# Local-and-global attention and a gated feed-forward on one core: key tiles of 120 + 8, stationary V, half-batches and hand-ordered streams in place of key blocks of 128, whole batches and the tool's order

## Chip, cores and metric

One core of one Trainium2 chip. The metric is the device time in microseconds of one execution, as the median of several; each comparison runs the two kernels in turn on the same chip. A profile is one execution with the hardware profiler; its span is some 1.7 us shorter than that execution's time.

## The reference

```python
# q, k, v: [4 batches, 8 heads, 768 tokens, 64]; n_global = 8, n_local = 96
scores = q @ k.T / 8
keep   = (key < 8) | (0 <= query - key < 96)
bias   = -slope[h] * (96 if global and not local else |query - key|)
a      = softmax(where(keep, scores + bias, -1e9))
x      = (a @ v), as [3072 tokens, 512]
out    = (relu(x @ w_gate) * (x @ w_val)) @ w_out     # 512 -> 1536 -> 512
```

Inputs and output are float32; both kernels compute in bfloat16 with float32 sums. The bias enters as a product with a table of exponentials after the exponential of the score, and the row sum comes from ones beside V, in the same matmuls as the values.

## The kernel before

Attention runs by batch and head pair. Scores of a 128-key block against the 256 queries that can see it go into one PSUM bank with a second block; the values come from `es` as the stationary operand and V (with a column of ones) as the moving one, so x has tokens on partitions and is transposed back. The feed-forward runs in chunks of 512 tokens, each as soon as its batches are done.

```python
f1g_psum = tile_pool(name="f1g", bufs=1, space=PSUM)      # one bank each
f1v_psum = tile_pool(name="f1v", bufs=1, space=PSUM)
f2_psum  = tile_pool(name="f2ps", bufs=1, space=PSUM)
# ... cut
for hp in range(H // 2):
    attention_pair(b, hp, x_sb, qkts[hp], vss[hp])
    # ... loads cut
    if hp < len(ffn_chunks):
        ffn_chunk(ffn_chunks[hp])                          # a whole chunk after one pair
bridge_batch(b, x_sb)                                      # transposes x
# ... cut; in ffn_chunk:
for fc in range(12):
    psg = f1g_psum.tile(...); psv = f1v_psum.tile(...)
    # 4 matmuls of 512 columns into psg, 4 into psv
    nc.scalar.activation(grelu, psg, Relu)
    nc.vector.tensor_tensor(ht[:, fc, :], psv, grelu, op=mult)
for tt in range(4):
    ps2 = f2_psum.tile(...)                                # 12 matmuls of 512 columns
    nc.scalar.copy(osb, ps2)
```

The chunks that become ready number 1, 2, 1 and 2 after batches 0 to 3, so batch 1 and batch 3 have one chunk beside their attention, and the last two chunks run alone.

The softmax here doesn't subtract the row's maximum and nothing guards it: scores larger than these inputs give would overflow.

## Time and profile before

| | before |
|---|---|
| time, median of 4 | 338.35 us |
| span of the profiled run | 339.5 us |
| busy: TensorE, VectorE, ScalarE, GpSimd | 298.9, 159.2, 127.2, 75.3 us |
| mean granted clock | 0.95 |
| DMA packets, bytes | 81,159, 20.77 MB |

Read it so: TensorE is the engine that the others serve, but its busy time is the sum of overlapping and modelled matmul durations, so 88% busy does not say that 12% is all there is to gain. The prediction below therefore builds a floor from the distances between the starts of matmuls, and shows the lines. The profiled execution is not one of the four timed: with a span of 339.5 us it took some 341, so it was about 1% slower than the median.

### The profile page before, as it was taken

The numbers are of one execution on the slowest core, as the hardware profiler recorded it, in microseconds if no ns is written. First come the engines' busy times: TensorE is split into PE (matmuls) and PEld (weight loads), VectorE is DVE, ScalarE is ACT, GpSimd is POOL, SyncE is SP. The second block draws the span as 40 slices with busy tenths as digits, with TensorE's granted clock in tenths as the row PEclk, the third lists the DMA queues.
The fourth block names the chain that finished last, engine by engine and source line by source line (L and its number), as shares of the span: only waits on it lengthen the run. The fifth ranks groups of instructions, "written<-read, shape, count | busy, mean of one in ns | idle before, by whom it ended". The sixth has DMA issues, their size and how long they took to land.

```text
span 339.5 us, 4809 instructions
## 1 busy us (share of the span) xinstructions
PE 298.9 (88%) x1858; PEld 145.1 (43%) x1888; DVE 159.2 (47%) x405; ACT 127.2 (37%) x233; POOL 75.3 (22%) x93
## 2 busy tenths in 40 slices
PE   0499878899997698999899997999998799999984
PEld 0254454544444354444444454544444343444431
DVE  8977676444258555422533266833366233113300
ACT  3356605232366242234332562432565133223311
POOL 9993192998011611000100000000000000000000
PEclk9999999599999959999999999999995599999999
DMA  6999999999317973001400110000210000020011
GB/s 41 118 136 200 195 163 181 150 140 132 78 62 48 71 47 23 0 33 62 56 0 2 64 61 2 0 2 0 75 50 0 2 0 1 32 93 1 0 57 69
DMA packets 81159, 20.77 MB, mean 61 GB/s; under 512 B 75504, under 2 KB 77040, under 8 KB 81136
## 3 DMA queue, kind: packets, MB, share of 16 engines
q0 software_dynamic: 77680, 14.16, 51.6%
q1 hardware_dynamic: 3456, 6.29, 5.0%
q8 instruction: 15, 0.25, 0.3%
q14 instruction: 8, 0.07, 0.1%
HBM read 28.31 MB, written 6.29 MB: 102 GB/s over the span
## 4 chain that ended last, share of the span: by engine, by line
PE 69%; DMA 10%; POOL 8%; DVE 5%; issue 4%; ACT 2%; DVEq 0%; POOLq 0%; ACTq 0%
PE f1v_ps L305 20%; PE f_ps L316 18%; PE f1g_ps L299 16%; DMA wv_sb<-in_moe_w_val_dram 6%; PE qk_ps L190 4%; DMA qs<-in_q_dram 4%; POOL qs L79 3%; POOL ks L80 3%; PE qk_ps L195 3%; PE tp L100 2%; PE av_ps L222 2%; DVE ht L312 2%; ACT es L201 2%; POOL vs L82 2%; PE tp L256 1%
## 5 line engine op out<-in xcount | busy, mean ns | idle before, releaser
L312 DVE TENSOR_TENSOR ht<-f1v_ps,grelu 128x512 bf16<-128x512 f32 x72 | 49.7, 691 | 81.5 <-PE f1v_ps L305 77.1
L311 ACT ACTIVATE grelu<-f1g_ps 128x512 bf16<-128x512 f32 x72 | 43.0, 598 | 113.5 <-PE f1g_ps L299 102.7
L305 PE MATMUL f1v_ps<-xt_all,wv_sb 128*128 128x512 bf16 x276 | 77.9, 390 | 4.5 <-DVE ht L312 3.8
L299 PE MATMUL f1g_ps<-xt_all,wg_sb 128*128 128x512 bf16 x276 | 78.0, 392 | 3.2 <-DVE xt_all L261 1.9
L201 ACT ACTIVATE es<-qk_ps 128x512 bf16<-128x512 f32 (+1 forms) x128 | 67.7, 571 | 29.3 <-PE qk_ps L195 26.3
L316 PE MATMUL f_ps<-wo_sb,ht 128*128 128x512 bf16 x282 | 65.2, 379 | 2.3 <-ACT osb L321 2.1
L305 PEld LDWEIGHTS <-wv_sb 128*128 128x128 bf16 x288 | 28.2, 99 | 45.3 <-issue 22.6
L190 PE MATMUL qk_ps<-dst 64*128 64x256 bf16 x128 | 38.7, 317 | 5.0 <-ACT es L201 3.2
L316 PEld LDWEIGHTS <-ht 128*128 128x128 bf16 x288 | 27.9, 98 | 34.0 <-issue 2.9
L299 PEld LDWEIGHTS <-wg_sb 128*128 128x128 bf16 x288 | 28.4, 101 | 31.6 <-issue 4.3
L195 PE MATMUL qk_ps<-dst 64*128 64x256 bf16 (+1 forms) x128 | 37.1, 305 | 0.0
L321 ACT COPY osb<-f_ps 128x512 f32<-128x512 f32 x24 | 14.1, 586 | 56.6 <-PE f_ps L316 36.0
L79 POOL DMA_DIRECT2D qs<-in_q_dram x34 | 30.3, 891 | 15.5 <-DMA wo_sb<-in_moe_w_out_dram 6.8
L82 POOL DMA_DIRECT2D vs<-in_v_dram x16 | 17.3, 1080 | 65.8 <-PE av_ps L235 36.3
L80 POOL DMA_DIRECT2D ks<-in_k_dram x34 | 30.1, 888 | 6.8 <-DMA wg_sb<-in_moe_w_gate_dram 6.6
L222 PE MATMUL av_ps<-vs,es 128*128 128x65 bf16 x192 | 23.9, 215 | 2.3 <-DVE x_sb L246 2.0
L204 DVE TENSOR_TENSOR es<-es,m_gg 128x512 bf16<-128x512 bf16 x64 | 22.8, 382 | 5.4 <-ACT es L201 5.1
L204 DVE TENSOR_TENSOR es<-es,m_kg 128x512 bf16<-128x512 bf16 x32 | 13.4, 418 | 25.4 <-ACT es L201 24.9
L104 DVE COPY dst<-tp 128x768 bf16<-128x768 bf16 x32 | 17.7, 552 | 12.8 <-PE tp L100 12.8
L222 PEld LDWEIGHTS <-es 128*128 128x128 bf16 x192 | 15.8, 109 | 17.7 <-issue 6.6
L228 PE MATMUL av_ps<-vs,es 128*128 128x65 bf16 x160 | 21.3, 214 | 0.0
L100 PE MATMUL tp<-ident,qs 128*128 128x128 bf16 x96 | 10.4, 257 | 12.4 <-DMA qs<-in_q_dram 10.8
(40 smaller groups left out, 180.0 us busy)
## 6 DMA issues: line engine op xcount, KB each, us to landing
out_dram<-osb SPq DMA_DIRECT2D x24, 256.0 KB, 2.0
vs<-in_v_dram POOLq DMA_DIRECT2D x16, 192.0 KB, 4.8
qs<-in_q_dram POOLq DMA_DIRECT2D x30, 96.0 KB, 4.3
ks<-in_k_dram POOLq DMA_DIRECT2D x30, 96.0 KB, 4.2
wg_sb<-in_moe_w_gate_dram POOLq DMA_DIRECT2D x1, 1536.0 KB, 12.7
wv_sb<-in_moe_w_val_dram POOLq DMA_DIRECT2D x1, 1536.0 KB, 19.3
wo_sb<-in_moe_w_out_dram POOLq DMA_DIRECT2D x1, 1536.0 KB, 13.5
qs<-in_q_dram POOLq DMA_DIRECT2D x4, 48.0 KB, 2.6
```

Source lines behind the costliest of these rows:

```text
L79: nc.gpsimd.dma_start(out=qs[:, sl, e, :], in_=src_q[:, sl])
L80: nc.gpsimd.dma_start(out=ks[:, sl, e, :], in_=src_k[:, sl])
L190: nc.tensor.matmul(ps[:, 0:colsA], lhsT=kT[:, blkA[0] * 128 : blkA[0] * 128 + 128], rhs=qT[:, blkA[1] : blkA[2]], start=True, stop=False)
L195: nc.tensor.matmul(ps[:, colsA : colsA + colsB], lhsT=kT[:, blkB[0] * 128 : blkB[0] * 128 + 128], rhs=qT[:, blkB[1] : blkB[2]], start=Fals ...
L201: nc.scalar.activation(es[:, 0:cols], ps[:, 0:cols], AF.Exp, bias=0.0, scale=scale)
L204: nc.vector.tensor_mul(es[:, 0:cols].rearrange("p (a c) -> p a c", a=2), es[:, 0:cols].rearrange("p (a c) -> p a c", a=2), m2[:, h, 0:cols ...
L222: nc.tensor.matmul(dst(qt), lhsT=lhs, rhs=vsl[:, qt, :], start=(cnt[bank] == 0), stop=False)
L299: nc.tensor.matmul(psg, lhsT=wg_sb[:, dc, fc * 128 : (fc + 1) * 128], rhs=xt_all[:, dc, t0 : t0 + TCH], start=(dc == 0), stop=(dc == N_DC ...
L305: nc.tensor.matmul(psv, lhsT=wv_sb[:, dc, fc * 128 : (fc + 1) * 128], rhs=xt_all[:, dc, t0 : t0 + TCH], start=(dc == 0), stop=(dc == N_DC ...
L311: nc.scalar.activation(grelu, psg, AF.Relu, bias=0.0, scale=1.0)
L312: nc.vector.tensor_tensor(ht[:, fc, :], psv, grelu, op=ALU.mult)
L316: nc.tensor.matmul(ps2, lhsT=ht[:, fc, tt * 128 : (tt + 1) * 128], rhs=wo_sb[:, fc, :], start=(fc == 0), stop=(fc == N_FC - 1))
```

## The change

Intent, part by part:

- **Key tiles.** A tile holds 8 global and 120 local keys, so one score matmul per tile and head pair covers both kinds; q is laid out with the other head's half zero, so one matmul serves two heads.
- **V and ones stationary.** `es` streams past V; x comes out with features on partitions, as the feed-forward wants it. The transposes of x go. The row sum arrives on 64 partitions, and its reciprocal is made on ScalarE as exp(-log(sum)).
- **Half-batches of 384 tokens.** Attention of half c+1 is cut into pieces and spread between the feed-forward pieces of half c.
- **Rotating banks.** Gate, value and output groups share three banks in turn.
- **Hand-ordered streams.** `manual_schedule()`: each engine executes in the order in which the program names its instructions; before, the tool's scheduler chose.
- **Wide rows.** q and k come in as float32 in runs of 768 bytes (three tokens), through the SP queue, and are cast on GpSimd (q of half 0 on VectorE); before, GpSimd's queue cast while it moved runs of 64 elements.

```diff
+    QH = S // 2; NN = 3; KT = 128 - NG; NHALF = 2 * B
-    f1g_psum ... bufs=1;  f1v_psum ... bufs=1;  f2_psum ... bufs=1
+    ff_psum = tile_pool(name="ffps", bufs=3, space=PSUM)
+    ctx.enter_context(tc.manual_schedule())
...  (loads)
-                nc.gpsimd.dma_start(out=qs[:, sl, e, :], in_=src_q[:, sl])
+            nc.sync.dma_start(out=dst[:, h0:h1, :],
+                in_=src[b, h0:h1, half*QH:(half+1)*QH, :].rearrange("h (p n) d -> p h (n d)", n=NN))
...  (values: es stationary, V moving -> V stationary, es moving)
-                nc.tensor.matmul(dst(qt), lhsT=es[...], rhs=vsl[:, qt, :], ...)
+            nc.tensor.matmul(av3[:, :, a : a + w], lhsT=vb[:, j, z0 : z0 + 128], rhs=es[...], ...)
+        nc.scalar.activation(ln[o0:o0+64], av[d0:d0+64, 0:QH], AF.Ln)
+        if e == 1:
+            nc.scalar.activation(rc, ln, AF.Exp, scale=-1.0)
+            for e_ in range(2):
+                nc.vector.tensor_tensor(xT_of[s][r, p, :], av_of[s, p, e_][r, 0:QH], rc[r], op=mult)
...  (order of the attention pieces of one half)
+        return (C(0) + C(1) + T(0) + C(2) + T(1) + C(3) + QK(0) + T(2) + QK(1) + AV(0) + T(3) + QK(2) + AV(1)
+                + QK(3) + AV(2) + AV(3))
...  (after the attention of half 0)
+    nc.vector.memset(vbuf[1]..., 0x3F803F80)               # ones of the second V buffer
+    # zero columns of the key tiles: 12 small memsets
+    for c in range(NHALF):
+        if c + 2 < NHALF:
+            load_half(c + 2)
+        a_items, f_items = attention_pieces(c + 1), ffn_pieces(c)
+        # after each feed-forward piece, as many attention pieces as are due
```

C is a cast, T the transposes of one head pair, QK a bank of scores, AV one head's values. Cuts are marked by "...".

Words used below. A PSUM bank is a piece of the memory in which TensorE leaves its sums. A *half* is one half-batch; there are eight, numbered from 0. A *group* is the set of matmuls that fill one bank once. The *product* is VectorE's multiplication of a value group with the relu of its gate group; it empties the value bank. The *normalisation* is VectorE's multiplication of a head pair's values with the reciprocal of their row sums. A *fill* is a memset that writes constant ones or zeros into a buffer.

## The prediction

> **What bounds the kernel now.** I read the page's slices first, then the chain, the windows on either side of the first feed-forward matmul, the groups, and last the timelines of two stages.
>
> ```profile
> PE   0499878899997698999899997999998799999984
> PEclk9999999599999959999999999999995599999999
> DMA  6999999999317973001400110000210000020011
> ...
> PE 69%; DMA 10%; POOL 8%; DVE 5%; issue 4%; ACT 2%; DVEq 0%; POOLq 0%; ACTq 0%
> ```
>
> TensorE is busy nearly everywhere and makes up 69% of the chain; the other engines do not bound. But the first quarter is DMA-busy, and the granted clock falls to half in slices near 60, 120 and 255 us. The same split, cut where the first gate matmul begins (48.7 us):
>
> ```profile
> 0.00:48.00 48.00, 31.62 (x244) 18.41 (x246) 37.74 (x138) 21.38 (x41) 34.53 (x46) 1.00 1.51 140
> 48.00:339.50 291.50, 267.32 (x1619) 126.71 (x1645) 121.50 (x267) 105.84 (x192) 40.81 (x48) 0.94 0.42 48
> ```
>
> PE busy is not PE at its peak, so I made a floor from start-to-start times at full clock: 12 output matmuls of 512 columns take 2.59 us (0.2158 each), two neighbouring score matmuls of 256 columns start 0.11 us apart, value matmuls of 65 columns 0.030, and 128-column transposes I take as 0.056 (estimate, from the column rate). Floor before: feed-forward 864 x 0.2158 = 186.4; scores 61,440 columns 26.2; values 480 x 0.030 = 14.5; 288 transposes (q, k, and x back) 16.1; together 243. The span is 339.5, so 96 us is lost: about 34 before 48.7 us, 58 after, 3.6 of tail. How the middle loses it, in the last chunk, which runs alone:
>
> ```profile
> 320.95 1.03 PE L299 MATMUL f1g_ps<-xt_all,wg_sb 128*128 128x512 bf16 x4
> 321.22 0.69 DVE L312 TENSOR_TENSOR ht<-f1v_ps,grelu 128x512 bf16<-128x512 f32 x1 [1.18 <-PE f1v_ps L305]
> ...
> 325.62 0.59 ACT L321 COPY osb<-f_ps 128x512 f32<-128x512 f32 x1 [3.00 <-PE f_ps L316]
> ...
> 326.25 2.75 PE L316 MATMUL f_ps<-wo_sb,ht 128*128 128x512 bf16 x11 [0.68 <-ACT osb L321]
> ```
>
> One value bank: the value group may begin only after the product has emptied it. The pair repeats every 1.87 us against 8 x 0.2158 = 1.73, so 72 x 0.15 = 10 us. One output bank: after every 12 matmuls TensorE waits 0.68 us for the copy, up to 24 x 0.7 = 16 us where no attention fills it. The rest is attention of whole batches with only one chunk beside it (98 to 127 us, 198 to 219, 248 to 268), data waits near 60 and 120 us, and the half clock these bring.
>
> The start:
>
> ```profile
> DMA packets 81159, 20.77 MB, mean 61 GB/s; under 512 B 75504, under 2 KB 77040, under 8 KB 81136
> ...
> 27.64 0.95 POOL L79 DMA_DIRECT2D qs<-in_q_dram  x1
> 35.24 0.82 POOL L80 DMA_DIRECT2D ks<-in_k_dram  x1 [6.64 <-DMA wg_sb<-in_moe_w_gate_dram]
> ```
>
> Nearly all packets are small. And GpSimd's issue at 35.24 waits for the transfer issued eight issues earlier; so do those at 42.23 and 58.61. I read eight as the number it may have open.
>
> **What the Trainium skill says.** "TensorE: Matmul & The Clock Gate", "Back-to-back issue gap": N/2.4 + 2.5 ns per matmul; the trace's 0.2158 at N=512 agrees, so I use it for 384 columns (0.1625). The same page, "Part 1: The HAM clock gate": a TensorE idle for a window drops to half clock; the 5s in the clock row stand where TensorE has gaps, so this agrees. "DMA: Bandwidth & Descriptors", "Specifications": transfers want 512 bytes for full rate; here 118 GB/s in the slice of 128-byte q, k, v packets against 209 in that of weights, which agrees. "GPSIMD Engine Reference", "4.1 Engine selection": one-input work there is roughly at line rate; no run here shows it, and I need it for the casts.
>
> **The change, part by part.**
> *TensorE work.* Feed-forward: 8 halves x 96 matmuls x 0.1625 = 124.8, plus 288 output matmuls 62.2: unchanged. Scores: the tile overlaps give 200 + 232 token columns in units of three, for two heads 1,200 columns in a first half and 1,392 in a second; 41,472 in all, 17.3 us + 144 x 2.5 ns = 17.6 (8.6 less). Values: V is stationary, so the moving side is es, again 41,472 columns: 17.3 + 288 x 2.5 ns + the shortest at a floor = 18.4, that is 4 *more* than before. Transposes: x leaves attention already transposed, 192 remain, 10.7 (5.4 less). Floor after 234: only 10 us less. **The gain must come from the 96 us of loss.**
>
> *Steady state.* One half is 29.2 us of TensorE: feed-forward 23.4 (24 x 0.65 + 6 x 1.3), attention of the next half 5.9. Three rotating banks remove the two waits above: a group takes 0.65 us, and its bank returns after about 0.2 + 0.56, within two groups.
> Is another engine slower? From durations here (ACT 167 ns + 0.84 per element; DVE from PSUM f32 551 ns at 384, bf16 masks 352 ns at 384):
> ACT per half: 12 relu 5.9, 3 output copies 1.8, 12 exponentials 6.4, 8 logarithms 3.9, 4 reciprocals as exponentials 2.1, 4 k copies 1.7: 21.8.
> DVE: 12 products 6.7, 18 mask products 5.4, 8 q copies 2.8, small k copies 1.5, 8 normalisations 4.4: 20.8.
> Both below 29.2. But the 12 products lie in the first two thirds of a half: DVE there is 17.2 of 19.7 us, tight. One wait I can point to: the last two head pairs' value pieces stand one output piece (1.3 us) apart, with two banks; logarithm 0.49, exponential 0.52, two products 1.1 plus hand-overs need about 2.2: 0.9 us lost per half. With 0.7 for jitter: 30.8 per half. Seven halves: 215.6.
>
> *Start.* q and k now come through SP in 768-byte runs; the first two loads should land within 4 us. But order is kept: GpSimd issues 13 transfers (about 1 us each, as now) after VectorE has filled the V buffer (3,808 words; memsets of 64 and 128 words took 112 and 165 ns, so 3.2 us, done at about 4.3), and only then casts k. First cast at about 17 us, first transpose at 18. VectorE's fills, mask arithmetic (14 operations near 0.3) and q cast end near 12, so they hide. Then half 0 runs with nothing beside it, in ScalarE order: 12 exponentials 6.4, logarithms and reciprocals 6.0, k copies 1.7, 12 late mask exponentials of 216 elements at about 0.38 (4.6), waits between: some 23 us, to 41. Second-buffer fills on VectorE (about 4.5 us) then delay the first product; three banks cover 1.9: feed-forward starts in effect at 43.7. So **the start hardly shrinks** (48.7 before), although only half a batch is waited for.
>
> *End.* The last half alone, 23.6, then copy and store 3.6, as now.
>
> Sum: 43.7 + 215.6 + 23.6 + 3.6 = **286 us**.
>
> **Rivals.**
> (a) VectorE or ScalarE becomes the bound. For: 87% of the first two thirds; strict program order makes one late item stall both; casts on GpSimd may slow VectorE. Against: averages of 71 to 75%, and the present timeline shows back-to-back ScalarE operations at no extra cost. At 34 us per half: 309.
> (b) The start is longer: casts on GpSimd behind a stalled issue. For: the eight-open rule; the weight transfers took 12 to 19 us to land. Against: the 13th issue waits for a V load, not for weights. If it waited for weights, 10 us more: 296.
> (c) The hand order works almost perfectly: 29.5 per half, and half 0 overlaps better, start 36: 270.
> (d) Nothing gained: the present loss is hidden structure that returns as waits. I see no wait large enough; 50 us would have to come back.
>
> **Range and chances.** (a) and (b) pull up, (c) down; half (a) and half (b) give about 302. I choose 286, range 270 to 305. Being within 2% needs (a) and (b) both in full and more: faster 0.96, same 0.03, slower 0.01.
>
> **What will show it.** In the changed profile: gate and value groups 0.65 us apart, with no wait of TensorE on the product; 512-column output groups with no 0.68 wait; seven repeats of 30 to 32 us; clock row at 9 from the first feed-forward on; first transpose near 18 us behind GpSimd's k cast; first gate matmul near 41. Wrong if: TensorE idles behind VectorE or ScalarE for over 3 us in a half, the value matmuls start much further apart than columns/2.4, or ScalarE shows table loads beyond the first.

## The result

| | before | after |
|---|---|---|
| time, median of 4 | 338.35 us | 304.6 us |
| span of the profiled run | 339.5 us | 302.9 us |
| busy: TensorE, VectorE, ScalarE, GpSimd | 298.9, 159.2, 127.2, 75.3 us | 247.9, 169.1, 168.3, 60.9 us |
| DMA packets, bytes | 81,159, 20.77 MB | 51,208, 27.50 MB |

The ratio of fast runs is 0.899 (95% interval 0.896 to 0.903). A ratio here is the mean time of one kernel's fast runs over that of the other's in the same rounds, so it is not quite the ratio of the medians quoted. The time lies inside the range (270 to 305), at its upper edge, 18.6 us above the predicted 286; 1.7 of that is only that the prediction added up a span. So the mechanism held and two terms of the sum were too small; a second chip gave the changed kernel 307.8. Bytes are counted as written, so q and k, which now arrive as float32, count double; both kernels read 28.3 to 28.4 MB.

Slices, and the first line of the chain, of the kernel after:

```profile
PE   0025351998899889989898989988998899899995
PEclk9999999999999999999999999999999999999999
DMA  3999999905192614432760518001700110001002
...
PE 69%; DVE 12%; ACT 10%; POOL 3%; DMA 3%; issue 3%; ACTq 0%; POOLq 0%
```

From the ninth slice on the TensorE row has no lump and the clock row no 5. The first eight slices are worse than before. In the chain GpSimd and DMA have given place to VectorE and ScalarE. The same cut in time as the prediction's, for the kernel after (columns: stretch, its length, busy time of TensorE, weight loads, VectorE, ScalarE, GpSimd, clock, DMA, GB/s):

```profile
0.00:48.00 48.00, 16.03 (x84) 9.48 (x84) 27.33 (x76) 19.72 (x47) 14.67 (x25) 1.00 1.12 200
48.00:302.90 254.90, 231.84 (x1581) 138.51 (x1596) 141.80 (x402) 148.57 (x314) 46.27 (x80) 1.00 0.35 70
```

TensorE did half as much in the first 48 us as before, and 254.9 us remain instead of 291.5. The last half, which runs alone, from TensorE's timeline of the kernel after:

```profile
289.50 0.81 PE L363 MATMUL ff_ps<-xT,wvB 128*128 128x384 bf16 x4
290.15 0.81 PE L353 MATMUL ff_ps<-xT,wgB 128*128 128x384 bf16 x4
290.81 0.81 PE L363 MATMUL ff_ps<-xT,wvB 128*128 128x384 bf16 x4
291.45 7.93 PE L372 MATMUL ff_ps<-wo_sb,ht 128*128 128x512 bf16 x35
```

Groups of four start 0.65 us apart, four times the 0.1625 that the prediction took, and all output matmuls follow in one run of 7.9 us without the 0.68 us wait. TensorE stands at its floor here.

**The books.** First gate matmuls of halves 1, 2 and later start at 84.64, 116.35, 148.39, ... 275.86 us: a mean period of 31.87 us. One period before 84.64 is 52.8, the start of half 0's feed-forward "in effect": when it would have begun had half 0 run at that period. With the prediction's floors:

| loss against TensorE's floor, us | before | after |
|---|---|---|
| start (to 48.7 / 52.8, less the attention's floor of 14.2 / 5.4) | 34.5 | 47.4 |
| middle | 58 | 18 |
| tail | 3.6 | 3.7 |
| floor itself | 243 | 234 |

So the 36.6 us of span come from the middle (-40) and the floor (some -9), and the start gives 13 back. The medians differ by 33.75 only; the other 3 us lie in the slow profile of the kernel before.

### The profile page after: what moved, and what is told of

Read it like the earlier page. It is cut to its first block, busy times and chain, and to the rows that moved or that the text cites. A ratio compares the mean times of both kernels' runs of the same rounds, so it can differ in the third digit from the quotient of the medians.

```text
span 302.9 us, 4741 instructions
## 1 busy us (share of the span) xinstructions
PE 247.9 (82%) x1665; PEld 148.0 (49%) x1680; DVE 169.1 (56%) x477; ACT 168.3 (56%) x361; POOL 60.9 (20%) x105
## 2 busy tenths in 40 slices
DMA packets 51208, 27.50 MB, mean 91 GB/s; under 512 B 27952, under 2 KB 46896, under 8 KB 51184
## 4 chain that ended last, share of the span: by engine, by line
PE 69%; DVE 12%; ACT 10%; POOL 3%; DMA 3%; issue 3%; ACTq 0%; POOLq 0%
PE ff_ps L372 20%; PE ff_ps L363 18%; PE ff_ps L353 17%; DVE xT L331 6%; PE av_ps L314 5%; PE qk_ps L286 5%; PE tp L245 3%; DMA vbuf<-in_v_dram 3%; ACT lnd L323 2%; ACT grelu L356 2%; ACT rcp L328 2%; POOL vbuf L135 2%; DVE ht L365 1%; DVE qp L251 1%; DVE vbuf L399 1%
## 5 line engine op out<-in xcount | busy, mean ns | idle before, releaser
L372 PE MATMUL ff_ps<-wo_sb,ht 128*128 128x512 bf16 x273 | 67.2, 379 | 0.8
L365 DVE TENSOR_TENSOR ht<-ff_ps,grelu 128x384 bf16<-128x384 f32 x96 | 53.1, 554 | 24.3 <-PE ff_ps L363 21.6
L331 DVE TENSOR_TENSOR xT<-av_ps,rcp 64x384 bf16<-64x384 f32 x64 | 35.5, 555 | 46.2 <-ACT rcp L328 33.5
L356 ACT ACTIVATE grelu<-ff_ps 128x384 bf16<-128x384 f32 x96 | 47.3, 493 | 24.3 <-DVE ht L365 13.8
L353 PE MATMUL ff_ps<-xT,wgB 128*128 128x384 bf16 x256 | 52.0, 325 | 4.8 <-DVE ht L365 4.8
L363 PE MATMUL ff_ps<-xT,wvB 128*128 128x384 bf16 x256 | 52.0, 325 | 3.5 <-ACT grelu L356 3.5
L289 ACT ACTIVATE es<-qk_ps 128x432 bf16<-128x432 f32 (+2 forms) x96 | 49.1, 538 | 4.0 <-PE qk_ps L286 3.2
L298 DVE TENSOR_TENSOR es<-es,m_all 128x432 bf16<-128x432 bf16 (+6 forms) x144 | 40.6, 314 | 18.1 <-ACT es L289 17.0
L286 PE MATMUL qk_ps<-qp,kT 128*128 128x432 bf16 (+6 forms) x144 | 33.6, 303 | 7.9 <-ACT es L289 7.9
L323 ACT ACTIVATE lnd<-av_ps 64x384 f32<-64x384 f32 x64 | 31.0, 485 | 12.8 <-PE av_ps L314 11.1
L234 POOL CAST qk<-qs 128x384 bf16<-128x384 f32 x28 | 14.3, 510 | 101.0 <-DMA qs<-in_q_dram 35.0
## 6 DMA issues: line engine op xcount, KB each, us to landing
wvB<-in_moe_w_val_dram POOLq DMA_DIRECT2D x1, 1024.0 KB, 29.5
```

Source lines behind the costliest of these rows:

```text
L286: nc.tensor.matmul(ps[:, c : c + n_], lhsT=kt[:, j, :], rhs=qd[:, :, :, a : a + w], start=True, stop=True)
L289: nc.scalar.activation(es[:, 0:cols], ps[:, 0:cols], AF.Exp, bias=0.0, scale=scale)
L298: nc.vector.tensor_mul(e4, e4, mk)
L323: nc.scalar.activation(ln[o0 : o0 + 64], av[d0 : d0 + 64, 0:QH], AF.Ln, bias=0.0, scale=1.0)
L331: nc.vector.tensor_tensor(xT_of[s][r, p, :], av_of[s, p, e_][r, 0:QH], rc[r], op=ALU.mult)
L353: nc.tensor.matmul(psg[:, 0:QH], lhsT=wg_of(dc, fc), rhs=xT[:, dc, :], start=(dc == 0), stop=(dc == N_DC - 1))
```

## Experiments

Each was run with a profile and three rounds against the kernel before on the same chip. The chips differ by a per cent. Kernels e1 to e4 share one chip, c0 to e7 another, e8 to e11 a third. All gave correct results. In c0 to e7 only two of the seven executions of the kernel before were fast, so ratios rest on two. The program that judges the runs calls the change and e8 to e11 faster, and c0 and e1 to e7 unclear; of all the intervals only that of e4 holds 1.

### What held the start

GpSimd's timeline of the kernel after:

```profile
17.21 1.02 POOL L152 DMA_DIRECT2D wo_sb<-in_moe_w_out_dram  x1 [0.85 <-DMA vbuf<-in_v_dram]
18.23 0.96 POOL L234 CAST qk<-ks 128x384 bf16<-128x384 f32 x2
20.08 0.96 POOL L234 CAST qk<-ks 128x384 bf16<-128x384 f32 x2 [0.90 <-DMA ks<-in_k_dram]
48.20 0.62 POOL L124 DMA_DIRECT2D vbuf<-in_v_dram  x1 [27.15 <-DVE vbuf L399]
48.81 3.61 POOL L135 DMA_DIRECT2D vbuf<-in_v_dram  x4
52.42 0.52 POOL L234 CAST qk<-qs 128x384 bf16<-128x384 f32 x1
```

and TensorE's, of the same kernel:

```profile
45.41 1.49 PE L353 MATMUL ff_ps<-xT,wgA 128*128 128x384 bf16 x4
52.99 0.94 PE L245 MATMUL tp<-ident,qk 128*128 128x128 bf16 x6 [6.09 <-POOL qk L234]
```

The first k cast came at 18.2 us, behind all 13 transfers, as foreseen. But then GpSimd stood for 27 us: its next instruction loads V of batch 1, and that waits for VectorE to fill the second V buffer, which the program names after the whole attention of half 0. The casts of half 1 stand behind that load, and TensorE idles 6.1 us for them.

**e1_early_fill.** The fills moved ahead of the first head pair:

```diff
     for h in range(2): build_masks(h)
+    nc.vector.memset(vbuf[1]..., 0x3F803F80); 12 small memsets
     pieces = attention_pieces(0)
     ...
-    nc.vector.memset(vbuf[1]..., 0x3F803F80); 12 small memsets
```

> The changed kernel with the second V buffer and the zero columns of the key tiles filled ahead of the first head pair instead of after the last one, in the stretch from 13 to 19 us where VectorE stands idle. Theory (the 8 us that the start lost against the prediction come from GpSimd's stream: the casts of half 1 stand behind a V load that waits for this fill, so TensorE idles 6.1 us at 47 us and the first product is late by some 3): 304.6 falls by 8 to 9, to about 296. Rival 1 (the start is bound by transfers; the slices are DMA-busy until 55 us): another wait takes its place, on q, k or weights, and it falls by under 3. Rival 2 (the fill itself on VectorE is the cost): falls by 3 to 4 only.

Measured 299.07 us, ratio 0.887 (0.879 to 0.895) against 0.899; span 297.0 against 302.9. That is 4 us by the ratios and 6 by the spans, less than the 8 to 9 expected. The idle is gone: the half-1 transposes start at 48.32 with no wait. But in this run the first k cast came at 19.94, not 18.23, since GpSimd's last two weight transfers waited 3.7 us for V loads to land instead of 1.6. With that 1.7 us the sum is 7.6. GpSimd's timeline of this run also shows what else can stand there:

```profile
26.88 0.93 POOL L135 DMA_DIRECT2D vbuf<-in_v_dram  x1 [3.03 <-DMA wvA<-in_moe_w_val_dram]
46.56 0.92 POOL L135 DMA_DIRECT2D vbuf<-in_v_dram  x1 [4.90 <-DMA wvB<-in_moe_w_val_dram]
53.88 0.64 POOL L135 DMA_DIRECT2D vbuf<-in_v_dram  x1 [6.39 <-DMA wo_sb<-in_moe_w_out_dram]
```

Each waits for the transfer that GpSimd issued eight issues earlier, the rule that the prediction read from the kernel before.

**e2_casts_ahead.** The fill stays late; only GpSimd's order changes:

```diff
     for c in range(NHALF):
+        if c == 0:
+            for p_ in range(HP): piece_cast(1, p_)         # and not again later
         if c + 2 < NHALF: load_half(c + 2)
```

> The changed kernel with only the order on GpSimd altered: the four casts of half 1 stand ahead of the V loads of half 2; the fill stays late on VectorE. Theory (order on GpSimd is the larger part, the fill's own 4 us on VectorE the smaller): the 6.1 us idle shrinks to 1 or 2, and the time falls by 4 to 5, to about 300. Rival (order is not the cause): within 1 us of 304.6.

Measured 301.23, ratio 0.895 (0.886 to 0.903); span 299.2, with the first k transposes 1.1 us later than in the kernel after. The 6.1 us idle is down to 0.4, and the rest of the fill's cost stays. As expected in kind; the intervals of e1 and e2 overlap, so the few us between them rest on the traces. They can be sized there: counted from the first gate matmul, the feed-forward starts in effect 11.4 us later in the kernel after, 6.1 in e2 and 3.7 in e1, at a period of 31.9 us in all three. So the order on GpSimd cost 5.3 us and the late fill itself 2.4. The last 3.7 stay in e1: a first group whose fourth matmul waits 1.3 us for the last normalisation, and groups at half pace.

**e5_narrow_rows.** Wide rows undone, in three loads of 256-byte runs each:

```diff
-            nc.sync.dma_start(out=dst[:, h0:h1, :], in_=....rearrange("h (p n) d -> p h (n d)", n=NN))
+            for n in range(NN):
+                nc.sync.dma_start(out=dst[:, h0:h1, n*D:(n+1)*D], in_=....rearrange("h (p n) d -> n p h d", n=NN)[n])
```

> The changed kernel with only the wide rows undone: each load of q or k is cut into three of 256-byte runs to the same places (three times the packets, the same bytes). Theory (transfers of the start are close to its bound: the k cast of heads 4 to 7 already waits for its data at 20 us): the first transposes and the casts of half 1 come 2 to 6 us later, and the time rises by 3 to 8. Rival (the start hangs on GpSimd's issues and ScalarE's chain, and later loads are a whole half ahead): under 1.5 us.

Measured 306.17, ratio 0.912 (0.903 to 0.921), beside 307.78 and 0.916 (0.902 to 0.930) for the unaltered control on that chip. The packets rose from 51,208 to 84,616, and k of heads 4 to 7 came later, as the theory said. The first casts began at 18.19 us, but in GpSimd's timeline of e5 the next two read:

```profile
26.50 0.96 POOL L235 CAST qk<-ks 128x384 bf16<-128x384 f32 x2 [7.35 <-DMA ks<-in_k_dram]
```

In the control the four casts run through from 19.18 with no such wait; its first cast is 1 us later because a weight transfer stood behind a V load. Little of the 7.35 us reaches TensorE: the first gate matmul starts at 43.19 against 42.28, and no difference shows in the time. So the rival was right about the time, the theory only about the transfers. The wide rows bought no time that these runs can show.

**c0_after_again**, the control:

> The changed kernel unaltered, as a control on the chip of the next three: every theory expects 304.6 within about 2 us; what it shows otherwise is the difference of chips, which the others are then held against.

307.78 us, 3 above the first chip's.

### What held the middle

VectorE in one half of the kernel after (timeline):

```profile
257.08 0.55 DVE L365 TENSOR_TENSOR ht<-ff_ps,grelu 128x384 bf16<-128x384 f32 x1
259.19 1.14 DVE L331 TENSOR_TENSOR xT<-av_ps,rcp 64x384 bf16<-64x384 f32 x2 [1.56 <-ACT rcp L328]
260.37 0.56 DVE L365 TENSOR_TENSOR ht<-ff_ps,grelu 128x384 bf16<-128x384 f32 x1
```

and TensorE there:

```profile
259.95 0.37 PE L286 MATMUL qk_ps<-qp,kT 128*128 128x144 bf16 x2
260.98 0.81 PE L353 MATMUL ff_ps<-xT,wgB 128*128 128x384 bf16 x4 [0.66 <-DVE ht L365]
```

Read it from below: TensorE waits 0.66 us for a bank that a value product has to empty. That product starts at 260.37, although its matmuls (from 257.67, four times 0.1625) were done near 258.4. It stands behind the normalisation of head pair 0, which in turn waits 1.56 us for ScalarE's reciprocal. VectorE is not full: it idles in front of the thing that it could do. In the first two thirds of this half (243.82 to 265.19) it is busy 14.3 of 21.4 us, 67%, not the 87% that I had estimated.

**e7_late_norm.** The normalisation of head pairs 0 and 1 becomes a piece of its own, named after the next attention piece:

```diff
-                + AV(0) + T(3) + QK(2) + AV(1) + QK(3) + ...
+                + AV(0) + then(T(3)[0], N(0)) + QK(2) + AV(1) + then(QK(3)[0], N(1)) + QK(3)[1:] + ...
```

> The changed kernel with the normalisation of head pairs 0 and 1 put one piece later in VectorE's stream, behind the next value product, nothing else. Theory (in each half TensorE loses 0.66 and 0.45 us to products and relus that stand behind a normalisation which itself waits 1.6 us for ScalarE's reciprocal): these two waits go, 0.8 to 1.4 us in each of seven halves: the control falls by 5.5 to 10. Rival (VectorE is simply full in the first two thirds of a half, 17.2 of 19.7 us as estimated): the waits move and the time falls by under 2.

Measured 296.37, 11.4 us below the control (ratio 0.883, 0.874 to 0.891, beside 0.916) and 10.1 by the spans, a little more than the 5.5 to 10 expected. The period falls from 31.88 in the control to 30.4 us. TensorE's waits, first the kernel after, then e7 (total us, times, longest):

```profile
PE av_ps L314 <- DVE xT L331: 6.6, 11, 1.7
PE ff_ps L353 <- DVE ht L365: 4.8, 7, 0.7
PE ff_ps L363 <- ACT grelu L356: 3.5, 7, 0.6
```

```profile
PE av_ps L314 <- DVE xT L335: 7.2, 12, 1.7
...
PE ff_ps L361 <- ACT grelu L364: 0.2, 1, 0.2
```

The waits on the product, one in each of seven halves, are gone, and of those on the relu a single one is left. The theory holds, and VectorE as a bound falls. The view counts idle time only after a matmul's modelled end; from start to start the two waits delay TensorE by 1.4 us in one kind of half and 1.6 in the other, and 1.5 is what the period loses.

**e6_auto_order.** Only the hand order undone:

```diff
-    ctx.enter_context(tc.manual_schedule())
```

> The changed kernel with only the hand order undone: the tool's own scheduler orders the streams. Theory (even spacing of attention pieces beside the feed-forward is what took some 40 us out of the middle, where the kernel before had attention in lumps): the time rises by 10 to 40, with TensorE idle in lumps. Rival (three banks and short pieces are enough, and the hand order even costs something through its late casts on GpSimd): 295 to 308.

Measured 285.28 us, ratio 0.845 (0.812 to 0.878; wide, since most runs of the kernel before on that chip were slow). My theory said 10 to 40 us slower; it is 22 us *faster* than the control. The theory had mixed two things. The order in which the program *names* the pieces, attention spread between feed-forward, is still there in e6. What is gone is only the rule that each engine must follow it. VectorE in e6, at the same place in a half:

```profile
121.77 0.56 DVE L364 TENSOR_TENSOR ht<-ff_ps,grelu 128x384 bf16<-128x384 f32 x1 [1.06 <-ACT lnd L322]
122.34 1.12 DVE L330 TENSOR_TENSOR xT<-av_ps,rcp 64x384 bf16<-64x384 f32 x2
```

The scheduler puts the value product ahead of the normalisation, as e7 does by hand. Two first gate matmuls of e6, halves 1 and 2:

```profile
77.51 0.85 PE L352 MATMUL ff_ps<-xT,wgA 128*128 128x384 bf16 x4
106.98 0.83 PE L352 MATMUL ff_ps<-xT,wgA 128*128 128x384 bf16 x4
```

Its period is 29.5 to 30.0 us against a floor of 29.2, and the start in effect is 77.51 - 29.7 = 47.8 against 52.8; 7 x 2.2 + 5 = 20 us, the whole difference between the spans, 283.0 and 302.9. The scheduler also puts the second fill (13.80 us) before the first q copies (28.18 us).

**e9_hand_both_cures.** The edits of e1 and e7 together, in hand order:

> The hand order with the two single cures together: the early fill and the late normalisation. Theory (the distance between hand order and automatic order is these two causes, one in the start and one in every half, and they add): 304.6 to 307 less 6 and less 9: 289 to 292, within some 6 us of the automatic order. Rival (they overlap, or the automatic order gains by something else): above 294.

Measured 291.08, ratio 0.861 (0.854 to 0.868); span 289.5. By spans, e1 saved 5.9 us against the kernel after and e7 10.1 against the control; the two together would be 16.0, and are 13.4 to 15.5, by which of the two they are held against. They add within 3 us, and most of the distance to the automatic order is these two causes: 15.5 of the 22.0 us of span between the control and e6, though e9 ran on another chip.

**e4_two_banks.** `bufs=3` of the feed-forward pool made 2:

> The changed kernel with two instead of three rotating banks for the feed-forward. Theory (the third bank absorbs the evacuation: a group takes 0.65 us, its bank returns about 0.85 us after its end, so two banks lose 0.1 us a group where nothing fills it, and each late item costs a group's 0.65 us more): 304.6 rises by 15 to 35, to about 328. Rival (late items on VectorE and ScalarE are what holds TensorE, and a bank more or less hardly matters): rises by under 6.

Measured 334.1, ratio 0.994 (0.983 to 1.005): the gain of the whole change is lost with the third bank. In its last half, alone, gate and value groups start 0.65 and 0.88 us apart by turns, 0.115 a group more than with three banks (expected 0.1), and the period grows to 35.2 us.

### Where the 40 us of the middle came from: the kernel before, altered

**e3_before_three_banks.** The three single banks of the kernel before become one pool of three:

```diff
-    f1g_psum, f1v_psum, f2_psum: bufs=1 each
+    ff_psum = tile_pool(name="ffps", bufs=3, space=PSUM)
```

> The kernel BEFORE with one part of the change alone: gate, value and output groups take turns on three PSUM banks instead of owning one each. Theory (part of what the change gained is the removed waits for single banks, 72 x 0.15 us at the value product and up to 24 x 0.7 us at the output copy): 338 falls to 317 to 326. Rival (these waits are filled by attention or come back elsewhere, and the gain was attention spread evenly beside the feed-forward): 333 to 338.

Measured 330.65, ratio 0.977 (0.963 to 0.991): 7.5 us, between the theory's 12 to 21 and the rival's 0 to 5. In the trace the waits for single banks are gone (TensorE waits 2.0 us in all for a product, in one place), but the clock row still has its 5s. That profile is of an execution in the slow state (clock 0.943), but the fast ones are at 0.953 to 0.956 too. Where the feed-forward runs through faster, the attention that follows has less beside it; that is how I read it, and e11 tests it. A part of the overestimate could have been read beforehand: in the kernel before, the output copy held TensorE in three places only, 2.1 us in all, where the prediction allowed up to 16.

**e11_before_spread.** Then, on top of e3, a chunk handed out in equal parts after the four head pairs:

```diff
-            if hp < len(ffn_chunks):
-                ffn_chunk(ffn_chunks[hp])
+            for f in pieces[len(pieces) * hp // 4 : len(pieces) * (hp + 1) // 4]:
+                f()
```

> The kernel BEFORE with three rotating banks (as in the earlier run, 330) and the feed-forward pieces that stand beside a batch's attention handed out in four equal parts, one after each head pair, instead of a whole chunk after one pair. Theory (lumps of attention with nothing beside them are the larger part of the middle's loss, with half-clock stages after them; the change's gain is mostly the even spread): 308 to 322, clock row without its 5s in the middle, but the last two chunks still run alone. Rival (the tool's scheduler already fills where it can, the gain comes from the smaller units and stationary V): 326 to 332.

Measured 309.5, ratio 0.918 (0.911 to 0.925). The window after 48 us and the clock row of e11:

```profile
48.00:308.30 260.30, 249.64 (x1616) 121.04 (x1644) 121.54 (x267) 106.03 (x192) 41.58 (x49) 0.99 0.47 54
```

```profile
PEclk9999999979999999999999999999999999999999
```

With 128-key blocks, moving V, narrow rows and whole batches, two small edits reach 0.918 where the rewrite has 0.899 to 0.916. Even spread is worth 21 us after the banks' 7.5 (some 20 by the ratios, as the two ran on different chips). What the rewrite adds beyond that is used up, in hand order, by its start and its in-order waits. It shows when they are gone: 285 and 279 in automatic order.

### Towards a better version

**e8_auto_k_on_vector.** Automatic order, and one word more:

```diff
-            eng = nc.vector if s == 0 and i == 0 else nc.gpsimd
+            eng = nc.vector if s == 0 else nc.gpsimd
```

> The automatic order of the run before, and the k casts of half 0 on VectorE as its q casts are, instead of on GpSimd behind its 13 transfers. In the automatic order the first k cast came at 27 us. Theory (that cast holds the start): first transposes of k near 12 to 14 us, the first feed-forward group some 5 to 8 us earlier, time 285 falls to 275 to 280. Rival (weights and q, k of heads 4 to 7, which land at 20 to 47 us, hold the start in its place): under 3 us.

Measured 279.18 (fast runs 277.6 to 279.5), ratio 0.827 (0.822 to 0.833): the fastest of all, as expected. The first transposes of both q and k start at 10.94 us instead of 27.64; the feed-forward starts in effect at 70.38 - 29.7 = 40.7, 7 us earlier than in e6. TensorE now waits at the start for V loads (4.3 us) and for the first value weights (1.8 us), so the rival has a part of the rest.

**e10_hand_all_cures.** All cures in hand order, and half 0 in two groups of head pairs:

```diff
+        if s == 0:
+            return (C(0) + C(1) + T(0) + T(1) + QK(0) + QK(1) + AVN(0) + AVN(1) + C(2) + T(2) + C(3) + T(3)
+                    + QK(2) + QK(3) + AVN(2) + AVN(3))
+        # other halves as in e7, with AV(2) among QK(3) and N(2) after its last bank
+    # fill by nc.gpsimd.memset at the very start; k casts of half 0 on VectorE; k copies reordered
```

> The hand order with all that the traces suggest: late normalisation; value pieces of head pairs 2 and 3 apart; the fill on GpSimd at the very start; k casts of half 0 on VectorE; pairs 0 and 1 of half 0 first, since heads 4 to 7 land at 20 us, with the mask exponentials between; small k copies ahead of ScalarE's. Theory: first feed-forward group near 35 us instead of 41, TensorE waits under 0.8 us in a half: 272 to 280. Rival (transfers bind the start once the casts are gone): 281 to 286.

Measured 293.84, ratio 0.869 (0.864 to 0.875): a miss, and no better than e9 (291.08; the intervals overlap). The transposes do start at 13.0, but the first gate matmul comes at 39.3, not near 35. VectorE's timeline of e10 shows where it stood, though no run tests this reading:

```profile
26.17 1.14 DVE L340 TENSOR_TENSOR xT<-av_ps,rcp 64x384 bf16<-64x384 f32 x2 [1.85 <-ACT rcp L333]
27.34 0.36 DVE L239 CAST qk<-qs 128x384 bf16<-128x384 f32 x1
27.62 0.35 DVE L239 CAST qk<-ks 128x384 bf16<-128x384 f32 x1
```

The casts of head pair 2 run without a wait of their own as soon as the normalisation in front of them has ended. I had put them behind it: the very mistake that e7 had cured, made again elsewhere. Even so the start is better than e9's: in effect 46.0 us against 49.7. Against e9 the loss is in the halves. Their period is 30.8 to 31.5 us, 0.9 more than e9's 30.4, not under 30. The new place of the value pieces made TensorE's wait for the normalisation longer, 1.07 us in a half where e7 has 0.62; that is about half of the 0.9, and the rest I did not trace. Neither rival nor theory had this.

## Why the prediction was right, and where it was short

- **What bounds** (TensorE with lumps, bank waits and a slow start): right. e3, e4 and e11 show both mechanisms of the middle in numbers. Its reading of the half clock agrees only in part: before the stretch near 60 us TensorE had idled 2.4 us for data, but before the one that begins near 254 us it had not idled longer than 0.52 us at once for 25 us. In e11, without the lumps, the 5s are gone; what lowers the clock no run separates.
- **Floor**: right. 0.65 us a group, the last half 23.4 us (predicted 23.6), tail 3.7 (3.6). The gain came from losses, not from less work, as stated. The prediction leaves out that the section of the Trainium skill that it cites for N/2.4 + 2.5 ("TensorE: Matmul & The Clock Gate", "Back-to-back issue gap") calls this the gap of an isolated matmul and gives some 131 ns for N=512 in a stream; here the formula held in streams too, with 0.2158 us at 512 columns. My 26 us for the bank waits was an upper bound; alone they gave 7.5, and the even spread, which I had not sized by itself, 21.
- **Operation costs**: right within 5% in sum for relus, logarithms, reciprocals, products and copies. The GpSimd cast took 0.51 us.
- **Start, first part**: right to about one microsecond (k cast foreseen at 17, was 18.2; first gate matmul at 41, was 41.4).
- **Start, second part** ("feed-forward starts in effect at 43.7"): short by 9.1 us. I had seen the second fill on VectorE and its delay of the product, but not who else waits for it: V's load on GpSimd, and behind that, in order, the casts. 6.1 us are that idle, and the product's delay runs inside it; by e2 and e1 the order on GpSimd cost 5.3 us and the fill 2.4, for which the sum had 2.7. Another 2.4 are four groups before and after the idle that ran at half pace, about 1.28 us each instead of 0.65, which the sum did not contain. Nor did it contain the first group's wait of 1.3 us for the last normalisation.
- **Per half** ("with 0.7 for jitter: 30.8"): short by 1.07, seven times, 7.5 us. The wait for the last pairs' value banks (foreseen 0.9) was there, 0.6 to 0.8 with a second, shorter one behind it. What I called jitter is two definite waits, 0.66 to 0.72 and 0.45 to 0.58 us, from one cause, and e7 removes them. From start to start the value banks cost 1.1 us in a half and the two waits 1.5; with the 29.2 of the floor that is 31.8, the measured period. So of its signs "no wait of TensorE on the product" failed, while groups 0.65 us apart, repeats of 30 to 32 us and a clock row of 9 came.
- 286 + 9.1 + 7.5 is 302.6, the span of 302.9.
- **Rivals**: (a) named the right danger, "strict program order makes one late item stall both", beside a wrong cause, a VectorE at 87%. Its other reason, casts on GpSimd that slow VectorE, did not show: a product beside such a cast took 0.55 us (at 55.47), as predicted without one. (b), "casts on GpSimd behind a stalled issue", came too, with nearly its 10 us, but what stalled was a later V load, behind a fill and not behind weights, and the casts were those of half 1. That "half (a) and half (b) give about 302" is so near the span of 302.9 is luck: neither came for its own reason. (c), an order that works almost perfectly, is nearly what the automatic order does: 29.7 per half. (d) did not occur.
- The Trainium skill's rule on runs of 512 bytes ("DMA: Bandwidth & Descriptors", "Specifications") led me to value the wide rows for the start; in e5, with 256-byte runs, k of heads 4 to 7 did come later, but it did not bind the time of this kernel.

Left open: how much of the remaining start, some 40 us in e8, the order of the transfers could still give; and how much each of stationary V, the 120 + 8 tiles and the half-batches is worth by itself. No run separated these.

## What to carry to other kernels

Keep the good part of a hand order, the sequence in which pieces of two stages are named, and let the scheduler move single instructions past a late one; if the order must be strict, look on every in-order engine for an instruction that waits while the next one could run, DMA issues and buffer fills included. Give an accumulator pool one bank more than two where groups are short, and spread the latency-bound stage evenly beside the dense one: in the old kernel these two small edits were worth nearly as much as the rewrite. An estimate of busy share says little about such waits; ask for each item what stands in front of it.

## What the Trainium skill lacked or had wrong

- "DMA: Bandwidth & Descriptors": I found no limit there on the transfers that GpSimd may have open. In both kernels, where a GpSimd issue waits for an earlier transfer, it is the one eight issues before it (6.6, 6.2 and 6.8 us before; 4.90 and 6.39 in e1). Whether chip or tool sets the eight, no run shows.
- "DMA: Bandwidth & Descriptors", "Specifications", 512 bytes: not wrong, but no guide to gain where loads are ahead: 256-byte runs in place of 768 made one cast wait 7.35 us for its data and left the time the same (306.2 and 307.8 us).
- "TensorE: Matmul & The Clock Gate", "Part 1": half pace was there (four 384-column matmuls in 1.28 us near 45 us, 0.65 later), while the profile's clock row read 9 and its mean 0.998; in the control's profile the row reads 5 there. The page warns that clock events are unreliable; the distances between matmul starts are the better witness.
- "GPSIMD Engine Reference", "4.1 Engine selection", one-input work at roughly line rate: a cast of 128x384 float32 to bfloat16 took 0.51 us on GpSimd and 0.34 on VectorE, so GpSimd took half as long again.
- None of the pages that I read tells what a strict program order costs beside the tool's own: here 20 us of 303 by the spans of the kernel after and e6, 22 against the control.
